# Delta-rule attention followed by a rational feed-forward layer: VectorE's steps of a unit in two fixed blocks of three, and three first halves per chunk made on ScalarE

## The chip, the core and the metric

The kernel runs on one core of a Trainium2 chip. The number that counts is the device time of one execution in microseconds (us). Of the kernel before, three runs are shown: 850.73, 851.33 and 855.22 us, so a median of 851.33 us. The profiled execution took 851.73 us.

The engines are named as in the profile: PE (TensorE, matrix products), DVE (VectorE), ACT (ScalarE), POOL (GpSimd) and SP (SyncE, which issues most DMAs). Each works through its own instructions in the order in which they were put there, and waits at an instruction until what that one needs is there.

## What is computed

Four batches with eight heads of 768 tokens and 48 numbers each go through a delta rule; the result, as 3072 tokens of 384 numbers, goes through a feed-forward layer with a rational function in the middle.

```python
k_n = k / (np.linalg.norm(k, axis=-1, keepdims=True) + 1e-06)
for t in range(S):
    kt, vt, bt = (k_n[:, :, t], v[:, :, t], beta[:, :, t, None])
    y[:, :, t] = np.einsum('bhd,bhde->bhe', q[:, :, t], state)
    v_old = np.einsum('bhde,bhd->bhe', state, kt)
    state = state + bt[:, :, :, None] * np.einsum('bhd,bhe->bhde', kt, vt - v_old)
...
h = x @ w_in
P = a[0] + a[1] * h + a[2] * h2 + a[3] * h3
Q = 1.0 + np.abs(b[0]) * np.abs(h) + np.abs(b[1]) * h2
g = P / (Q + 1e-06)
return (g @ w_out).astype(np.float32)
```

## The kernel before, in words

**Chunks.** The 768 tokens are cut into 12 chunks of 64. Within a chunk the delta rule is solved with matrix products; from chunk to chunk a state is carried. Four functions of a chunk run side by side on different chunks: `ahead` (loads, keys normalized), `front` (products of keys, the inverse of a triangle by small steps on DVE, products of queries), `middle` and `back` (the solution, the next state, the outputs, the tokens for the feed-forward layer). "Attention" below means all of them.

**Two halves.** Numbers that go into a product are kept as two numbers of 16 bits: a first half, which is the number rounded, and a second half, which is the rest. `split16` makes both. In the kernel before, three of its calls in each chunk give the first half to POOL (argument `hi`, L226): for the keys and for the queries (`transposed`, tile `kn`, one buffer that both use in turn) and for the key products (`key_products`, tile `gl`). The second half of these three is a subtraction on POOL (L232). The halves in `kn` go out to DRAM by a DMA (`xdk` for keys, `xdq` for queries), and the next first half may only be written into `kn` when that DMA has read it.

**Units.** The feed-forward layer of a chunk has 8 units of 256 inner columns, so there are 96 units. `hidden(n)` makes a bank of 512 columns in PSUM (tile `ph`, two buffers) with 18 matrix products (L806). `numerator(n)` and `quotient(n)` apply the rational function to it, and `accumulate(n)` multiplies it with `w_out` (L869). Letters for the steps of a unit, used from here on:

- ACT: z (L824, from PSUM), u (L828, from PSUM), |w| (L829), Ln (L842), Exp (L843)
- DVE, each with one input in PSUM and one in SBUF: W (L826, from z and `ph`), U (L830, from u and `ph`), V (L831)
- DVE, each with both inputs in SBUF: G (L848, or L846 where POOL has helped), X (L849), Y (L853)
- POOL: the last product of a unit (L854) in all 96; in 36 units (chunks 2 to 10, units 0, 4, 5 and 6 of each) also L835, just after V, and L851, in place of Y

z(n) comes before W(n), that before u(n) (ACT waits for it in the built program, since both read the same bank), u(n) before U(n), then V(n), G(n) (which also needs Exp(n)), X(n), Y(n) and L854(n).

**Order.** The main loop writes `numerator(n)`, then `quotient(n - 1)`, then a piece of attention, `accumulate(n - 2)` and `hidden(n + 1)`. That order is only a priority: a scheduler that runs when the kernel is built picks for each engine, by its own estimates of durations, the most urgent instruction that would be ready. It may therefore put U(n) behind X(n - 1), or attention between any two steps, and the order that it finds is fixed in the program.

Of the kernel before, what the change touches and what calls it, by code (L numbers as in the profile page):

```python
# [15 lines left out]
ALU = mybir.AluOpType  # L16
# [20 lines left out]
def kernel(  # L37
# [12 lines left out]
    nc = tc.nc  # L50
# [4 lines left out]
    C = 64  # L55
# [120 lines left out]
    def zeroed(n, shape, dtype, nm, part=lambda t: t, eng=nc.gpsimd):  # L176
        made = []
        for i in range(n):
# [14 lines left out]
            eng=nc.vector if nm in "kwe" else nc.gpsimd,  # L193
# [15 lines left out]
    def as_rows(ap, b):  # L209

        return (
            ap[b * C : (b + 1) * C]
            .rearrange("(m j) x -> m (j x)", j=NB)[:, : C * C]
            .rearrange("m (t s) -> t m s", s=C)
        )
# [4 lines left out]

    S16 = cpool.tile([P, HP, D], F32, name="S16")

    def split16(dst, src, scale=None, eng=None, hi=None):

        if hi is not None:
            hi.tensor_scalar(dst[0], src, 1.0 if scale is None else scale, 0.0, op0=ALU.mult, op1=ALU.add)  # L226
        elif scale is None:
            nc.scalar.copy(dst[0], src)  # L228
        else:
            nc.scalar.activation(dst[0], src, AF.Copy, scale=scale)  # L230
        if scale is None:
            (eng or nc.vector).tensor_sub(dst[1], src, dst[0])  # L232
        else:
            nc.vector.scalar_tensor_tensor(  # L234
                out=dst[1], in0=src, scalar=scale, in1=dst[0], op0=ALU.mult, op1=ALU.subtract
            )
# [94 lines left out]
    def load_in(i):  # L331
        w64 = moe_w_in.bitcast(U32)
        t = w_out[:, i].rearrange("p a b e -> p (a b e)").bitcast(U32).rearrange("p (c f) -> p c f", c=NCC)
        for cc in range(NCC):
            to_f32(t[:, cc], w64[cc * P : (cc + 1) * P, i * 4 * P : (i + 1) * 4 * P], f"i{i}_{cc}")
        s2 = w_in[:, i, 0].bitcast(BF16)
        nc.scalar.activation(s2, t.bitcast(F32), AF.Square)
        pf = ps_h.tile([P, 2 * P], F32, tag="h", name=f"pfw{i}")
        for cc in range(NCC):
            nc.tensor.matmul(pf, ones16, s2[:, cc], start=cc == 0, stop=cc == NCC - 1)  # L340
        ss = sb.tile([P, 1], F32, tag="ss", name=f"wss_{i}")
        nc.vector.tensor_reduce(sw[:, 2, i : i + 1], pf, axis=AX.X, op=ALU.max)
# [69 lines left out]
    def bank(pool, nm, w):  # L412

        t = pool.tile([P, NPAIR, 512], F32, tag="a", name=nm)[:, :, : H * w].rearrange("x p (h w) -> x p h w", w=w)
        return t[:, 0], t[:, 1], t

    def by_pair(t):

        return t.rearrange("x (p h) d -> x p h d", p=NPAIR)
# [30 lines left out]
    def transposed(x, src, nm, soon):  # L450


        split16(
            [x[:, i, :, :, :D].rearrange("p h b d -> p b h d") for i in range(2)],
            src.rearrange("p (b h) d -> p b h d", b=2),
            eng=nc.gpsimd,
            hi=nc.gpsimd,
        )
        xd = dpool.tile([NPAIR, 2, NH, C, HG, 2, DP], F16, tag="xd" + nm[0], name=f"xd{nm}", bufs=4 if nm[0] == "k" else 2)
        for p in PAIRS:  # L460
            nc.sync.dma_start(
                out=xd[p].rearrange("i n t a b d -> t (i n) (a b d)"),
                in_=x[p * C : (p + 1) * C].rearrange("t i (n a) b d -> t (i n) (a b d)", n=NH),
            )
        t = sb.tile([P, NPAIR, 2, NH, C, HG], F16, tag="tt", name="t" + nm)
        if soon:
            pts = ps_f.tile([P, 2, H, P], F16, tag="a", name=f"pt{nm}")
            for i in range(2):
                pt = pts[:, i]
                for h in range(H):  # L470
                    nc.tensor.transpose(pt[:, h], x[:, i, h].rearrange("p b d -> p (b d)"), ident16)
                for p in PAIRS:
                    nc.scalar.copy(
                        t[:, p, i].rearrange("x n t a -> x n a t"),
                        pt[:, :, p * C : (p + 1) * C].rearrange("x (n a) t -> x n a t", a=HG),
                    )
            return t, xd
        nc.sync.dma_start(
            out=t.rearrange("x p i n t a -> x (p i n t a)"),
            in_=xd.rearrange("p i n t a b d -> (p i n t a) (b d)"),  # L480
            transpose=True,
        )
        return t, xd
# [29 lines left out]
    def key_products(c):  # L513
        d = info[c]
        gd = d["gd"] = dpool.tile([P, BS], F32, tag="gd", name=f"gd_{c}")
        pg = bank(ps_f, f"pg_{c}", C)
        mm3(pg, d["kbd"], d.pop("tk"))
        g = sb.tile([P, HP, C], F32, tag="g", name=f"g_{c}", bufs=1)
        nc.scalar.mul(by_pair(g), pg[2], -1.0)
        for b in range(2):  # L520
            nc.sync.dma_start(out=as_rows(gd, b), in_=g[b * C : (b + 1) * C])
        gl = sb.tile([P, HP, C - 16, 2], F16, tag="gl", name=f"gl_{c}", bufs=1)
        split16([gl[..., i] for i in range(2)], g[:, :, : C - 16], eng=nc.gpsimd, hi=nc.gpsimd)
        d["gl"] = gl

    def inverse(c):
# [110 lines left out]
    def queries_transposed(c):  # L637
        d = info[c]
        qt = d.pop("qt")
        scaled(qt, d["sq"])  # L640
        d["tq"] = transposed(kn_b, qt, f"q_{c}", c == 0)[0]
# [151 lines left out]

    unit = {}
    acc = {}
    obs = {}

    def hidden(n):
# [17 lines left out]
    def numerator(n):  # L816

        c, f2 = divmod(n, NU)
        d = unit[n]
        A3, B1, A1, B0, A0, Q0 = (toks[c]["m"][:, i, f2 : f2 + 1] for i in range(6))  # L820
        ph = d.pop("ph")

        r = z = sb.tile([P, 2, TG], F32, tag="mr", name=f"mr{n}", bufs=MB)
        nc.scalar.activation(z, ph, AF.Abs, scale=B1)  # L824
        w = sb.tile([P, 2, TG], F32, tag="mw", name=f"mw{n}", bufs=MB)
        nc.vector.scalar_tensor_tensor(out=w, in0=z, scalar=B0, in1=ph, op0=ALU.add, op1=ALU.mult)  # L826
        u = sb.tile([P, 2, TG], F32, tag="mu", name=f"mu{n}", bufs=MB)
        nc.scalar.activation(u, ph, AF.Identity, scale=A3, bias=a2)  # L828
        nc.scalar.activation(w, w, AF.Abs)  # L829
        nc.vector.tensor_mul(u, ph, u)  # L830
        nc.vector.scalar_tensor_tensor(out=u, in0=u, scalar=A1, in1=ph, op0=ALU.add, op1=ALU.mult)  # L831

        by_pool = 2 <= c < NCH - 1 and f2 in (0, 4, 5, 6)
        if by_pool:
            nc.gpsimd.tensor_scalar(u, u, A0, 1.0, op0=ALU.add, op1=ALU.mult)  # L835
        d.update(u=u, w=w, r=r, A0=A0, Q0=Q0, by_pool=by_pool)

    def quotient(n):

        d = unit[n]  # L840
        u, w, r, A0, Q0, by_pool = (d.pop(x) for x in ("u", "w", "r", "A0", "Q0", "by_pool"))
        nc.scalar.activation(r, w, AF.Ln, bias=Q0)  # L842
        nc.scalar.activation(r, r, AF.Exp, scale=-1.0)  # L843
        g = sb.tile([P, 2, 2, TG], F16, tag="mg", name=f"mg{n}", bufs=MB)
        if by_pool:
            nc.vector.tensor_mul(g[:, 0], u, r)  # L846
        else:
            nc.vector.scalar_tensor_tensor(out=g[:, 0], in0=u, scalar=A0, in1=r, op0=ALU.add, op1=ALU.mult)  # L848
        nc.vector.scalar_tensor_tensor(out=w, in0=w, scalar=Q0, in1=g[:, 0], op0=ALU.add, op1=ALU.mult)  # L849
        if by_pool:  # L850
            nc.gpsimd.tensor_sub(u, u, w)  # L851
        else:
            nc.vector.scalar_tensor_tensor(out=u, in0=u, scalar=A0, in1=w, op0=ALU.add, op1=ALU.subtract)  # L853
        nc.gpsimd.tensor_mul(g[:, 1], u, r)  # L854
        d["g"] = g

# [65 lines left out]
    def front(c, j):  # L922

        if j == 0:
            keys_transposed(c)
        elif j == 1:
            key_products(c)
        elif j == 2:
            invs[c] = inverse(c)
            next(invs[c])  # L930
            scales(c)
            queries_transposed(c)
        elif j == 3:
# [113 lines left out]
```

## Time and profile before

| | |
|---|---|
| median of three runs | 851.33 us |
| profiled execution | 851.73 us |
| its span, first to last instruction | 849.4 us |
| first W of unit 0 starts | 150.8 us |
| first W of the last chunk (unit 88) starts | 804.9 us |
| DMA queue of SP, share of 16 engines | 69.7% |
| granted TensorE clock, mean | 0.89 |

In a row of a group of instructions stand the line, the engine, the operation, what it writes and reads, the shape and the count; behind the first bar its busy time in us and the mean duration of one in ns; behind the second bar the idle time of the engine just before these instructions, and what ended most of it. In a row of the timeline stand the start and the duration in us, and in brackets the idle time before it and what ended that. The rows of stretches of time give, for each engine, its busy time and its count of instructions, then the granted clock, the share of the DMA engines that were busy and the GB/s.

### The profile page before, as it was taken

What the parts mean: (1) busy time and instruction counts of PE and PEld (TensorE: products, weight loads), DVE (VectorE), ACT (ScalarE), POOL (GpSimd) and SP (SyncE); (2) the same over time, 40 slices, a digit from 0 to 9 for tenths busy, and PEclk for the clock granted to TensorE, in tenths of its full rate; (3) what the DMA queues carried; (4) which work ended last, traced back from release to release, by engine and by line L of the source; (5) the groups of instructions that cost most, each with busy time, mean ns of one, the idle gap of its engine ahead of it and who ended that gap; (6) DMA issues with size and microseconds to landing.
All of it is one profiled execution on the core that took longest, in us unless ns stands there. A gap on an engine that the chain in (4) does not pass through costs nothing.

```text
span 849.4 us, 23212 instructions
## 1 busy us (share of the span) xinstructions
PE 625.6 (74%) x9264; PEld 491.3 (58%) x9264; DVE 761.0 (90%) x1369; ACT 589.5 (69%) x1242; POOL 466.9 (55%) x430
## 2 busy tenths in 40 slices
PE   0230425777788678888868869879879889999885
PEld 0220425656466467666756747657657767787563
DVE  5999898799799889889978898897999999999886
ACT  3766667748575675886774866767677867887774
POOL 7665665464436556565564655664756546454522
PEclk9855556988999899999999989989989999999999
DMA  8987989959899968959879498379587583300000
GB/s 230 259 198 148 221 157 172 149 117 148 155 172 147 175 123 160 151 102 193 144 140 176 85 183 149 66 158 165 89 159 129 97 139 58 72 2 20 1 20 19
DMA packets 466507, 111.46 MB, mean 131 GB/s; under 512 B 431328, under 2 KB 463072, under 8 KB 466400
## 3 DMA queue, kind: packets, MB, share of 16 engines
q1 hardware_dynamic: 464224, 108.83, 69.7%
q8 instruction: 72, 1.18, 0.6%
q10 hardware_dynamic: 2176, 1.17, 0.5%
q14 instruction: 35, 0.29, 0.1%
HBM read 40.47 MB, written 26.23 MB: 79 GB/s over the span
## 4 chain that ended last, share of the span: by engine, by line
DVE 41%; ACT 14%; DMA 12%; PE 11%; issue 8%; SPq 8%; POOL 3%; POOLq 0%; ACTq 0%; DVEq 0%
DVE mw L849 4%; PE ph L806 4%; PE po L869 4%; DVE w_out L327 3%; DVE mw L826 3%; DVE mg L848 3%; DVE mu L830 3%; DVE mu L831 3%; DVE mu L853 2%; ACT mu L828 2%; DVE mg L846 2%; SPq L609 2%; DVE z L234 2%; ACT mr L824 2%; ACT kp L764 2%
## 5 line engine op out<-in xcount | busy, mean ns | idle before, releaser
L806 PE MATMUL ph<-xT,w_in 128*128 128x256 f16 x1728 | 224.2, 283 | 37.1 <-DVE mu L831 33.8
L869 PE MATMUL po<-w_out,mg 128*128 128x384 f16 x1152 | 223.4, 339 | 33.5 <-POOL mg L854 27.3
L806 PEld LDWEIGHTS <-w_in 128*128 128x128 f16 x1728 | 172.0, 102 | 76.4 <-DVE mu L831 24.9
L854 POOL TENSOR_TENSOR mg<-mu,mr 128x512 f16<-128x512 f32 x96 | 135.3, 1410 | 106.5 <-DVE mu L853 50.9
L869 PEld LDWEIGHTS <-mg 128*128 128x128 f16 x1152 | 110.6, 101 | 105.5 <-POOL mg L854 34.1
L828 ACT ACTIVATE mu<-ph,coef,msc 128x512 f32<-128x512 f32 x96 | 74.7, 778 | 54.4 <-DVE mw L826 54.2
L849 DVE SCALAR_TENSOR_TENSOR mw<-mw,msc,mg 128x512 f32<-128x512 f32 x96 | 92.6, 965 | 0.5
L851 POOL TENSOR_TENSOR mu<-mu,mw 128x512 f32<-128x512 f32 x36 | 51.0, 1418 | 72.5 <-DVE mw L849 38.3
L824 ACT ACTIVATE mr<-ph,msc 128x512 f32<-128x512 f32 x96 | 64.9, 682 | 36.9 <-POOL mg L854 11.5
L403 PEld LDWEIGHTS <-kbd 128*128 128x128 f16 x1680 | 60.8, 104 | 35.2 <-issue 33.4
L826 DVE SCALAR_TENSOR_TENSOR mw<-mr,msc,ph 128x512 f32<-128x512 f32 x96 | 70.4, 737 | 10.7 <-ACT mr L824 10.6
L831 DVE SCALAR_TENSOR_TENSOR mu<-mu,msc,ph 128x512 f32<-128x512 f32 x96 | 70.8, 739 | 1.1
L830 DVE TENSOR_TENSOR mu<-ph,mu 128x512 f32<-128x512 f32 x96 | 65.2, 680 | 5.6 <-ACT mu L828 4.6
L842 ACT ACTIVATE mr<-mw,msc 128x512 f32<-128x512 f32 x96 | 69.4, 724 | 0.9
L403 PE MATMUL pu<-z,ebd 128*128 128x48 f16 x1728 | 52.7, 186 | 19.4 <-DVE z L234 15.4
L848 DVE SCALAR_TENSOR_TENSOR mg<-mu,msc,mr 128x512 f16<-128x512 f32 x60 | 58.9, 982 | 6.2 <-ACT mr L843 5.7
L403 PEld LDWEIGHTS <-ebd 128*128 128x128 f16 x1728 | 51.7, 98 | 22.0 <-issue 20.8
L843 ACT ACTIVATE mr<-mr 128x512 f32<-128x512 f32 x96 | 60.2, 630 | 0.7
L829 ACT ACTIVATE mw<-mw 128x512 f32<-128x512 f32 x96 | 60.0, 625 | 0.0
L853 DVE SCALAR_TENSOR_TENSOR mu<-mu,msc,mw 128x512 f32<-128x512 f32 x60 | 52.1, 869 | 0.2
L835 POOL TENSOR_SCALAR mu<-mu,msc 128x512 f32<-128x512 f32 x36 | 28.1, 782 | 40.5 <-DVE mu L831 28.3
L232 POOL TENSOR_TENSOR mm<-m,mm 128x1024 f16<-128x1024 f32 x12 | 31.1, 2589 | 32.7 <-ACT mm L228 30.5
(198 smaller groups left out, 1306.3 us busy)
## 6 DMA issues: line engine op xcount, KB each, us to landing
wsi<-in_moe_w_in_dram SPq DMA_DIRECT2D x24, 256.0 KB, 5.2
xdk<-kn SPq DMA_DIRECT2D x24, 256.0 KB, 3.7
kbd<-tk SPq DMA_DIRECT2D x24, 256.0 KB, 5.1
gd<-g SPq DMA_DIRECT2D x24, 256.0 KB, 3.5
wso<-in_moe_w_out_dram SPq DMA_DIRECT2D x32, 192.0 KB, 4.0
xdq<-kn SPq DMA_DIRECT2D x24, 256.0 KB, 3.6
mbd<-mm SPq DMA_DIRECT2D x24, 256.0 KB, 5.4
wc<-img SPq DMA_DIRECT2D x24, 256.0 KB, 4.8
```

What stands on the lines that cost most here:

```text
L403: nc.tensor.matmul(dst[p][:, h], head(bd, lp, p * H + h), head(rt, rp, p * H + h), start=start and n == 0 and h == 0, stop=stop and n == l ...
L806: nc.tensor.matmul(ph[:, i], w_in[:, f2, wp, cc, i * P : (i + 1) * P], x[:, xp, cc], start=k == 0, stop=k == 3 * NCC - 1,)
L824: nc.scalar.activation(z, ph, AF.Abs, scale=B1)
L826: nc.vector.scalar_tensor_tensor(out=w, in0=z, scalar=B0, in1=ph, op0=ALU.add, op1=ALU.mult)
L828: nc.scalar.activation(u, ph, AF.Identity, scale=A3, bias=a2)
L830: nc.vector.tensor_mul(u, ph, u)
L831: nc.vector.scalar_tensor_tensor(out=u, in0=u, scalar=A1, in1=ph, op0=ALU.add, op1=ALU.mult)
L842: nc.scalar.activation(r, w, AF.Ln, bias=Q0)
L848: nc.vector.scalar_tensor_tensor(out=g[:, 0], in0=u, scalar=A0, in1=r, op0=ALU.add, op1=ALU.mult)
L849: nc.vector.scalar_tensor_tensor(out=w, in0=w, scalar=Q0, in1=g[:, 0], op0=ALU.add, op1=ALU.mult)
L854: nc.gpsimd.tensor_mul(g[:, 1], u, r)
L869: nc.tensor.matmul(po[p], g[:, gp, i, p * P : (p + 1) * P], w_out[:, f2, wp, i], start=f2 == lo and i == 0 and k == 0, stop=f2 == hi - 1 a ...
```

## The change

The change does two things. The six DVE steps of a unit get a mark, by which the scheduler has to leave them in the order in which the program writes them: W, U, V of unit n, then G, X, Y of unit n - 1 (where POOL helps, there is no Y). Anything else may still be put between them. And the argument `hi` is gone, so that the three first halves per chunk are made by ACT; POOL keeps the second halves.

```diff
-    def split16(dst, src, scale=None, eng=None, hi=None):
-
-        if hi is not None:
-            hi.tensor_scalar(dst[0], src, 1.0 if scale is None else scale, 0.0, op0=ALU.mult, op1=ALU.add)
-        elif scale is None:
+    def split16(dst, src, scale=None, eng=None):
+
+        if scale is None:
             nc.scalar.copy(dst[0], src)
...
             src.rearrange("p (b h) d -> p b h d", b=2),
             eng=nc.gpsimd,
-            hi=nc.gpsimd,
         )
...
-        split16([gl[..., i] for i in range(2)], g[:, :, : C - 16], eng=nc.gpsimd, hi=nc.gpsimd)
+        split16([gl[..., i] for i in range(2)], g[:, :, : C - 16], eng=nc.gpsimd)
...
+    def in_order(bi):
+
+        tc.stamp_issue_order_token(bi.ins, "unit")
+
...
-        nc.vector.scalar_tensor_tensor(out=w, in0=z, scalar=B0, in1=ph, op0=ALU.add, op1=ALU.mult)
+        in_order(nc.vector.scalar_tensor_tensor(out=w, in0=z, scalar=B0, in1=ph, op0=ALU.add, op1=ALU.mult))
...
-        nc.vector.tensor_mul(u, ph, u)
-        nc.vector.scalar_tensor_tensor(out=u, in0=u, scalar=A1, in1=ph, op0=ALU.add, op1=ALU.mult)
+        in_order(nc.vector.tensor_mul(u, ph, u))
+        in_order(nc.vector.scalar_tensor_tensor(out=u, in0=u, scalar=A1, in1=ph, op0=ALU.add, op1=ALU.mult))
...
         if by_pool:
-            nc.vector.tensor_mul(g[:, 0], u, r)
+            in_order(nc.vector.tensor_mul(g[:, 0], u, r))
         else:
-            nc.vector.scalar_tensor_tensor(out=g[:, 0], in0=u, scalar=A0, in1=r, op0=ALU.add, op1=ALU.mult)
-        nc.vector.scalar_tensor_tensor(out=w, in0=w, scalar=Q0, in1=g[:, 0], op0=ALU.add, op1=ALU.mult)
+            in_order(nc.vector.scalar_tensor_tensor(out=g[:, 0], in0=u, scalar=A0, in1=r, op0=ALU.add, op1=ALU.mult))
+        in_order(nc.vector.scalar_tensor_tensor(out=w, in0=w, scalar=Q0, in1=g[:, 0], op0=ALU.add, op1=ALU.mult))
...
-            nc.vector.scalar_tensor_tensor(out=u, in0=u, scalar=A0, in1=w, op0=ALU.add, op1=ALU.subtract)
+            in_order(nc.vector.scalar_tensor_tensor(out=u, in0=u, scalar=A0, in1=w, op0=ALU.add, op1=ALU.subtract))
```

Two places show what the scheduler made of it. The first is DVE's order near the end, in the last chunk, where no attention is left; the digits behind `mw`, `mu` and `mg` are the unit's number. Before, it stood so:

```order
L826 SCALAR_TENSOR_TENSOR mw91_13902<-mr91_13900,msc_11_13624,ph_91_13881 128x512
L849 SCALAR_TENSOR_TENSOR mw90_13853<-mw90_13853,msc_11_13624,mg90_13911 128x512
L853 SCALAR_TENSOR_TENSOR mu90_13855<-mu90_13855,msc_11_13624,mw90_13853 128x512
L830 TENSOR_TENSOR mu91_13904<-ph_91_13881,mu91_13904 128x512
L831 SCALAR_TENSOR_TENSOR mu91_13904<-mu91_13904,msc_11_13624,ph_91_13881 128x512
L826 SCALAR_TENSOR_TENSOR mw92_13949<-mr92_13947,msc_11_13624,ph_92_13928 128x512
L848 SCALAR_TENSOR_TENSOR mg91_13958<-mu91_13904,msc_11_13624,mr91_13900 128x512
L849 SCALAR_TENSOR_TENSOR mw91_13902<-mw91_13902,msc_11_13624,mg91_13958 128x512
L830 TENSOR_TENSOR mu92_13951<-ph_92_13928,mu92_13951 128x512
```

With the change (whose lines have moved down by two: L828, L832, L833, L850, L851 and L855 are W, U, V, G, X and Y) the same place reads:

```order
L828 SCALAR_TENSOR_TENSOR mw91_13902<-mr91_13900,msc_11_13624,ph_91_13881 128x512
L832 TENSOR_TENSOR mu91_13904<-ph_91_13881,mu91_13904 128x512
L833 SCALAR_TENSOR_TENSOR mu91_13904<-mu91_13904,msc_11_13624,ph_91_13881 128x512
L850 SCALAR_TENSOR_TENSOR mg90_13911<-mu90_13855,msc_11_13624,mr90_13851 128x512
L851 SCALAR_TENSOR_TENSOR mw90_13853<-mw90_13853,msc_11_13624,mg90_13911 128x512
L855 SCALAR_TENSOR_TENSOR mu90_13855<-mu90_13855,msc_11_13624,mw90_13853 128x512
L828 SCALAR_TENSOR_TENSOR mw92_13949<-mr92_13947,msc_11_13624,ph_92_13928 128x512
L832 TENSOR_TENSOR mu92_13951<-ph_92_13928,mu92_13951 128x512
```

Between W and U of one unit there stood two steps of the unit before; now U is right behind W, and G has moved behind the V of the next unit. Over the whole program W and U have nothing between them in 22 of 96 units (before in 1) and a single instruction in 23 (before in 5). Pairs in which a step directly follows the one whose result it reads (U and V, G and X, X and Y) were 49 and are 115.

The second place is the first halves in `kn` for the queries of chunk 6 and the keys of chunk 7. Before, both stood in POOL's order, between the units' steps:

```order
L226 TENSOR_SCALAR kn0_109<-q_6_5318 128x2x8x48
L851 TENSOR_TENSOR mu24_5619<-mu24_5619,mw24_5617 128x512
L232 TENSOR_TENSOR kn0_109<-q_6_5318,kn0_109 128x2x8x48
L854 TENSOR_TENSOR mg24_5754<-mu24_5619,mr24_5615 128x512
L854 TENSOR_TENSOR mg25_6007<-mu25_5747,mr25_5743 128x512
L232 TENSOR_TENSOR rr_5_6277<-v_5_4061,rr_5_6277 128x768
L226 TENSOR_SCALAR kn0_109<-k_7_5424 128x2x8x48
```

With the change they stand in ACT's order (L826, L830, L831, L844 and L845 are now z, u, |w|, Ln and Exp):

```order
L226 CAST kn0_109<-q_6_5318 128x2x8x48
L826 ACTIVATE mr24_5615<-ph_24_5596,msc_3_5316 128x512
L826 ACTIVATE mr25_5743<-ph_25_5724,msc_3_5316 128x512
L830 ACTIVATE mu24_5619<-ph_24_5596,coef_99,msc_3_5316 128x512
L831 ACTIVATE mw24_5617<-mw24_5617 128x512
L844 ACTIVATE mr24_5615<-mw24_5617,msc_3_5316 128x512
L845 ACTIVATE mr24_5615<-mr24_5615 128x512
L226 CAST kn0_109<-k_7_5424 128x2x8x48
L830 ACTIVATE mu25_5747<-ph_25_5724,coef_99,msc_3_5316 128x512
```

The first half of the keys, which has to wait until the queries' DMA has left `kn`, is now in front of u of unit 25 on ACT.

## The prediction, made before the changed kernel ran

> **What bounds the kernel now.** I read the page's busy times first, then the chain that ended last, and then the stretches of time.
>
> ```profile
> span 849.4 us, 23212 instructions
> PE 625.6 (74%) x9264; PEld 491.3 (58%) x9264; DVE 761.0 (90%) x1369; ACT 589.5 (69%) x1242; POOL 466.9 (55%) x430
> DVE 41%; ACT 14%; DMA 12%; PE 11%; issue 8%; SPq 8%; POOL 3%; POOLq 0%; ACTq 0%; DVEq 0%
> ```
>
> DVE is busy for 90% of the span and has the largest share of the chain; ACT has 260 us of idle time, POOL 383. The stretches below are the chunks 0 to 8, the chunks 9 and 10, and the last chunk with the end.
>
> ```profile
> 150.80:721.30 570.50, 469.20 (x7366) 369.81 (x7365) 518.81 (x857) 398.30 (x810) 322.56 (x261) 0.93 0.79 138
> 721.30:804.90 83.60, 78.94 (x972) 61.00 (x969) 76.12 (x118) 67.98 (x135) 40.76 (x34) 1.00 0.11 25
> 804.90:849.40 44.50, 31.27 (x212) 20.61 (x210) 34.15 (x48) 26.59 (x43) 10.96 (x9) 0.93 0.07 18
> ```
>
> In the first of them DVE (third pair) works 91% of the time; in the second PE (94%) and DVE (91%) are both nearly full. So a microsecond more or less in DVE's queue is mostly one in the span. How much of DVE's time is work? The groups of the unit's steps answer that.
>
> ```profile
> L849 DVE SCALAR_TENSOR_TENSOR mw<-mw,msc,mg 128x512 f32<-128x512 f32 x96 | 92.6, 965 | 0.5
> L831 DVE SCALAR_TENSOR_TENSOR mu<-mu,msc,ph 128x512 f32<-128x512 f32 x96 | 70.8, 739 | 1.1
> L826 DVE SCALAR_TENSOR_TENSOR mw<-mr,msc,ph 128x512 f32<-128x512 f32 x96 | 70.4, 737 | 10.7 <-ACT mr L824 10.6
> L830 DVE TENSOR_TENSOR mu<-ph,mu 128x512 f32<-128x512 f32 x96 | 65.2, 680 | 5.6 <-ACT mu L828 4.6 <-POOL mm L232 0.7
> L848 DVE SCALAR_TENSOR_TENSOR mg<-mu,msc,mr 128x512 f16<-128x512 f32 x60 | 58.9, 982 | 6.2 <-ACT mr L843 5.7
> L853 DVE SCALAR_TENSOR_TENSOR mu<-mu,msc,mw 128x512 f32<-128x512 f32 x60 | 52.1, 869 | 0.2
> L846 DVE TENSOR_TENSOR mg<-mu,mr 128x512 f16<-128x512 f32 x36 | 32.7, 908 | 5.1 <-ACT mr L843 4.3 <-POOL mu L835 0.7
> L854 POOL TENSOR_TENSOR mg<-mu,mr 128x512 f16<-128x512 f32 x96 | 135.3, 1410 | 106.5 <-DVE mu L853 50.9
> L851 POOL TENSOR_TENSOR mu<-mu,mw 128x512 f32<-128x512 f32 x36 | 51.0, 1418 | 72.5 <-DVE mw L849 38.3
> ```
>
> W, U and V read `ph` in PSUM and take 737, 680 and 739 ns. G, X and Y, of the same size, read two tiles in SBUF and take 0.87 to 0.98 us. The timeline shows why.
>
> ```profile
> 641.95 2.37 POOL L232 TENSOR_TENSOR mm<-m,mm 128x1024 f16<-128x1024 f32 x1 [1.01 <-ACT mm L228]
> 642.02 2.85 DVE L849 SCALAR_TENSOR_TENSOR mw<-mw,msc,mg 128x512 f32<-128x512 f32 x1
> 649.10 0.73 DVE L849 SCALAR_TENSOR_TENSOR mw<-mw,msc,mg 128x512 f32<-128x512 f32 x1
> ```
>
> The same X takes 0.73 us, or 2.85 us when POOL began a subtraction 0.07 us earlier; then it ends 0.55 us after POOL does. So a DVE step with two SBUF inputs stands still while POOL runs, and one that reads PSUM doesn't. What this costs: X 96 x (0.965 - 0.74) = 21.6 us, L848 60 x (0.982 - 0.74) = 14.5, L853 60 x (0.869 - 0.74) = 7.7, L846 36 x (0.908 - 0.68) = 8.2; together **52 us**, the most that an order of the unit's steps can win there.
>
> A rule of the Trainium skill bears on this ("SBUF — State Buffer", section "SBUF: two separate sides"): VectorE and GpSimd share one pair of ports as an exclusive lock, and the loser is blocked for the other's whole instruction; on VectorE's side two SBUF inputs are enough to need it. The rows above agree (2.85 against 0.73 us). The rule speaks for blocks, since in a PSUM block POOL is free, and against them as well, since in a block of G, X, Y any POOL step that arrives gets in at a boundary and stops the next. With no collision left the sum below would be 32 us lower, which is the first rival's way.
>
> **The change part by part.** (a) *The unit's own POOL steps.* L854 follows Y, so after the change it runs beside W, U, V of the next unit, and L851 likewise. They are 135.3 + 51.0 = 186.3 us of the 374.3 us that POOL is busy in the three stretches, so by share 26 of the 52 us. I take **-20**, as the steps of attention are longer (2.37 us above) and stop DVE longer. Bounds 0 and -52.
>
> (b) *36 first halves leave POOL.*
>
> ```profile
> L226 POOL TENSOR_SCALAR gl<-g 128x768 f16<-128x768 f32 x12 | 13.4, 1119 | 8.4 <-ACT g L519 8.0
> L226 POOL TENSOR_SCALAR kn<-k 128x768 f16<-128x768 f32 x12 | 11.3, 944 | 21.1 <-DMA xdq<-kn 21.0
> L226 POOL TENSOR_SCALAR kn<-q 128x768 f16<-128x768 f32 x12 | 10.9, 912 | 0.7
> L228 ACT CAST rr<-v 128x768 f16<-128x768 f32 x12 | 9.9, 828 | 10.0 <-DVE v L679 10.0
> ```
>
> At the rate of (a), 26 us for 132 steps or 0.2 us each, that is **-7** (bounds 0 and -15).
>
> (c) *G no longer waits for Exp.* It now stands a unit later. Its 5.7 + 4.3 us of waits go: **-10** (bounds -5 and -10). Late next is z, for which W already waits 10.6 us.
>
> (d) *L835 gets between G and X.* It is released by V, and G(n - 1) is now the step behind V.
>
> ```profile
> 645.45 0.74 DVE L853 SCALAR_TENSOR_TENSOR mu<-mu,msc,mw 128x512 f32<-128x512 f32 x1
> 645.70 1.05 POOL L835 TENSOR_SCALAR mu<-mu,msc 128x512 f32<-128x512 f32 x1 [1.38 <-DVE mu L831]
> L835 POOL TENSOR_SCALAR mu<-mu,msc x36: 691/696/1408, 302.2 to 796.7; 128x512 f32<-128x512 f32 x36
> ```
>
> It came 0.25 us into a Y, waited for that (1.05 instead of 0.70 us) and ended 0.56 us behind it. X, which follows its G at once, would be held for about 0.33 us net, in 36 units: **+12** (bounds 0 and 36 x 0.70 = 25).
>
> (e) *DVE has nothing between W and U.* The timeline near the end shows the loop.
>
> ```profile
> 826.89 0.75 DVE L826 SCALAR_TENSOR_TENSOR mw<-mr,msc,ph 128x512 f32<-128x512 f32 x1 [0.45 <-ACT mr L824]
> 827.56 0.74 DVE L848 SCALAR_TENSOR_TENSOR mg<-mu,msc,mr 128x512 f16<-128x512 f32 x1
> 827.67 0.78 ACT L828 ACTIVATE mu<-ph,coef,msc 128x512 f32<-128x512 f32 x1 [0.81 <-DVE mw L826]
> 828.34 0.75 DVE L849 SCALAR_TENSOR_TENSOR mw<-mw,msc,mg 128x512 f32<-128x512 f32 x1
> 829.00 0.68 DVE L830 TENSOR_TENSOR mu<-ph,mu 128x512 f32<-128x512 f32 x1
> 829.60 0.74 DVE L853 SCALAR_TENSOR_TENSOR mu<-mu,msc,mw 128x512 f32<-128x512 f32 x1
> 830.92 0.74 DVE L826 SCALAR_TENSOR_TENSOR mw<-mr,msc,ph 128x512 f32<-128x512 f32 x1
> ```
>
> W ends at 827.64, u runs on ACT from 827.67 to 828.45, and G and X fill that time, so that a unit takes 830.92 - 826.89 = 4.03 us. In the new order U is next behind W: it can start at 828.49 at the earliest, 1.60 us after W, where the next step otherwise starts 0.66 us after the one before. That is 0.94 us lost, and all that stands behind U waits with it. In the built order 22 units have nothing in between (21 us) and 36 more have steps that by the trace's durations are shorter than 0.94 us, and lose 17 us; before, the same count gives 6 us. So **+31** (bounds +15, the empty ones less 6, and +45, where ACT is not free when W ends). 7.5 us of it lie in the last chunk, where nothing else is left to fill.
>
> (f) *Neighbours that depend on each other.* G at 827.56 ends at 828.30 and X, which reads it, starts 0.04 us later; X ends at 829.09, but U, which doesn't read it, starts 0.09 us before that. The difference is 0.12 us, and 66 such pairs are added: **+8** (bounds 0 and +8). The Trainium skill ("VectorE: DVE Perf Modes", section "The DRAIN you can't avoid") reports eight copies that took the same with a semaphore after each as with one at the end; by that (f) would be 0 and the sum 8 us lower. The trace has this difference, so I keep it.
>
> (g) *ACT's 36 first halves.* At 828 ns, the row for `rr`, they are 30 us, beside 260 us of idle time. But the 21.0 us that POOL waited for `xdq` to leave `kn` move to ACT with them, and behind the keys' half stands the u that DVE needs.
>
> ```profile
> 429.97 0.83 POOL L226 TENSOR_SCALAR kn<-q 128x768 f16<-128x768 f32 x1
> 442.45 0.83 POOL L226 TENSOR_SCALAR kn<-k 128x768 f16<-128x768 f32 x1 [3.35 <-DMA xdq<-kn]
> 491.93 0.82 POOL L226 TENSOR_SCALAR kn<-q 128x768 f16<-128x768 f32 x1
> 500.82 0.83 POOL L226 TENSOR_SCALAR kn<-k 128x768 f16<-128x768 f32 x1 [3.92 <-DMA xdq<-kn]
> ```
>
> From the queries' half to the free buffer it took 12.5 and 8.9 us. In the built order 4.5 to 6.9 us of ACT work lie between the two in seven chunks. DVE can go on for some 3 us with the steps of the unit before, so I take 2 us in each of seven: **+14** (bounds 0 and 11 x 3.6 = 40, the waits above in all eleven).
>
> (h) *Absorbed.* DVE idles 698.6 - 629.1 = 69.5 us in the three stretches, waiting for attention that doesn't run faster when DVE is late; a tenth of that swallows delay: **-7** (bounds 0 and -15). The first 150.8 us hold no unit; I count nothing for them.
>
> The sum: -20 - 7 - 10 + 12 + 31 + 8 + 14 - 7 = +21 us. The span becomes 849.4 + 21 = 870.4, and with the 2.3 us around it (851.73 - 849.4) **872.7 us**. The profiled execution is 0.4 us above the median of 851.33, so nothing has to be shifted.
>
> **The rivals.**
>
> *POOL's collisions vanish (faster).* If POOL's steps of attention also fall into the PSUM blocks, which (e) makes longer, (a) becomes three quarters of the 52 us, -39; a gap in which POOL works off its queue also spares collisions, so (d) is 0, (e) is 20 and (g) 8. The sum is -39 - 7 - 10 + 20 + 8 + 8 = -20: 832 us. For it speaks the size of the 52 us; against it, that releases of POOL's attention steps have no tie to the blocks. With the other terms as I took them, the sign turns where (a) passes 41 us.
>
> *They cancel (no change).* (a) -30 and (g) +6 with the rest as above give +3: 855 us.
>
> *ACT holds everything up.* (g) at its bound of 40 gives +47: 899 us. In order, ACT would stop u, z and Exp for each late DMA. DVE's slack of 3 us speaks against it.
>
> *The blocks don't do what they say.* POOL's steps run late and land in G, X, Y as often as before; (a) is 0: +41, 893 us.
>
> **How the numbers follow.** My forecast, 860 to 886 us, has a chance of 0.45; the faster rival 0.25; the cancelling one 0.13; ACT 0.10; the blocks without effect 0.07. The predicted time is 873 us. A measurement of this kernel can tell a change from none at about 0.5%, 4 us. Faster has 0.25, the same 0.13, slower 0.45 + 0.10 + 0.07 = 0.62. The range reaches from 832, the faster rival's time, to 897, short of the worst of ACT: about 0.12 and 0.07 are left out.
>
> **What would show it.** Right, if X's mean falls from 965 ns towards 800 and L854's idle time before it stays; if U's idle time, ended by u (L828), grows from 4.6 us to 30 or more; if a unit in the last chunk takes 5.2 us (1.60 + 0.72 + 0.66 + 0.78 + 0.78 + 0.66) instead of 4.03; if ACT's halves in `kn` show a wait for `xdq` of 14 us or more. Wrong, if U doesn't wait (ACT's u came without W, or the gaps were filled), if G, X and Y fall to 0.75 us all over, or if the chain turns to PE.

## The result, and the profile after

The changed kernel takes **878.42 us** (median of 4 runs, 876.82 to 880.06), beside 853.28 us for the kernel before (4 runs, the three shown above and one of 855.31 us): a ratio of 1.0321, 95% interval 1.0288 to 1.0353. It is slower, by 25 us. The forecast was 873.0 us, with 832 to 897 as its range. The traces are of single executions: 879.89 us for the changed kernel and 851.73 us for the kernel before, so their difference is about 3 us larger than that of the medians.

The page of the changed kernel, its span, its busy times and its chain:

```profile
span 878.2 us, 23202 instructions
PE 640.3 (73%) x9264; PEld 500.0 (57%) x9264; DVE 743.7 (85%) x1369; ACT 615.6 (70%) x1278; POOL 428.0 (49%) x394
DVE 40%; DMA 18%; PE 14%; SPq 10%; ACT 8%; issue 6%; POOL 2%; POOLq 0%; DVEq 0%; ACTq 0%
```

DVE works *less* than before (743.7 us, before 761.0) and still the span is 28.8 us longer: DVE's idle time went from 849.4 - 761.0 = 88.4 to 878.2 - 743.7 = 134.5 us, by 46.1. The groups of instructions say where; W, U, V, G, X, Y are now L828, L832, L833, L850 (with POOL's help L848), L851 and L855, and POOL's steps L837, L853 and L856.

```profile
L851 DVE SCALAR_TENSOR_TENSOR mw<-mw,msc,mg 128x512 f32<-128x512 f32 x96 | 88.3, 920 | 1.0
L828 DVE SCALAR_TENSOR_TENSOR mw<-mr,msc,ph 128x512 f32<-128x512 f32 x96 | 70.9, 739 | 1.7 <-ACT mr L826 1.6
L832 DVE TENSOR_TENSOR mu<-ph,mu 128x512 f32<-128x512 f32 x96 | 65.9, 686 | 47.1 <-ACT mu L830 43.0 <-POOL mg L856 2.3 <-POOL rr L230 1.6
L850 DVE SCALAR_TENSOR_TENSOR mg<-mu,msc,mr 128x512 f16<-128x512 f32 x60 | 48.2, 803 | 0.0
L855 DVE SCALAR_TENSOR_TENSOR mu<-mu,msc,mw 128x512 f32<-128x512 f32 x60 | 47.8, 797 | 1.1
L848 DVE TENSOR_TENSOR mg<-mu,mr 128x512 f16<-128x512 f32 x36 | 25.6, 711 | 0.0
L837 POOL TENSOR_SCALAR mu<-mu,msc 128x512 f32<-128x512 f32 x36 | 37.4, 1039 | 53.3 <-DVE mu L833 53.1
```

G, X and Y together took 92.6 + 58.9 + 52.1 + 32.7 = 236.3 us before and take 88.3 + 48.2 + 47.8 + 25.6 = 209.9 now: the collisions with POOL did fall, by 26.4 us. The idle time before U went from 5.6 to 47.1 us, that before W from 10.7 to 1.7, and that before G from 6.2 + 5.1 to nothing. That is +41.5 - 9.0 - 11.3 = +21.2 of the 46.1 us; the other 24.9 stand nearly all before steps of attention. Some of the waits (what waits, for what, us in total, times, longest) name them:

```profile
DVE mu L832 <- ACT mu L830: 43.0, 45, 2.9
...
ACT kn L226 <- DMA xdq<-kn: 25.7, 7, 7.8
...
DVE sc L617 <- PE pfq L247: 7.0, 5, 2.3
DVE nrm L492 <- ACT sq L491: 7.0, 4, 2.7
DVE xs L737 <- PE px L736: 6.0, 4, 2.0
...
DVE m L655 <- PE pm L401: 4.6, 5, 1.3
```

DVE waits for u in 45 units, about 0.96 us each. ACT's wait for the queries' DMA is the second row; what it costs DVE is a question for the runs. The last chunk's timeline shows the new loop:

```profile
856.91 0.74 DVE L828 SCALAR_TENSOR_TENSOR mw<-mr,msc,ph 128x512 f32<-128x512 f32 x1
857.68 0.78 ACT L830 ACTIVATE mu<-ph,coef,msc 128x512 f32<-128x512 f32 x1 [2.14 <-DVE mw L828]
858.57 0.69 DVE L832 TENSOR_TENSOR mu<-ph,mu 128x512 f32<-128x512 f32 x1 [0.92 <-ACT mu L830]
859.29 0.75 DVE L833 SCALAR_TENSOR_TENSOR mu<-mu,msc,ph 128x512 f32<-128x512 f32 x1
859.96 0.75 DVE L850 SCALAR_TENSOR_TENSOR mg<-mu,msc,mr 128x512 f16<-128x512 f32 x1
860.74 0.75 DVE L851 SCALAR_TENSOR_TENSOR mw<-mw,msc,mg 128x512 f32<-128x512 f32 x1
861.53 0.75 DVE L855 SCALAR_TENSOR_TENSOR mu<-mu,msc,mw 128x512 f32<-128x512 f32 x1
862.20 0.74 DVE L828 SCALAR_TENSOR_TENSOR mw<-mr,msc,ph 128x512 f32<-128x512 f32 x1
```

W, then u on ACT, then U, each after the other: 862.20 - 856.91 = 5.29 us a unit, where the kernel before took 4.03.

### The profile page after: what moved, and what is told of

The parts are those of the page before. It is cut to its first block, busy times and chain, and to the rows that moved or that the text cites. A ratio compares the mean times of both kernels' runs of the same rounds, so it can differ in the third digit from the quotient of the medians.

```text
span 878.2 us, 23202 instructions
## 1 busy us (share of the span) xinstructions
PE 640.3 (73%) x9264; PEld 500.0 (57%) x9264; DVE 743.7 (85%) x1369; ACT 615.6 (70%) x1278; POOL 428.0 (49%) x394
## 4 chain that ended last, share of the span: by engine, by line
DVE 40%; DMA 18%; PE 14%; SPq 10%; ACT 8%; issue 6%; POOL 2%; POOLq 0%; DVEq 0%; ACTq 0%
DVE mw L851 5%; PE ph L808 4%; DVE mu L833 4%; DVE mu L832 4%; PE po L871 4%; DMA k<-in_k_dram 3%; DVE mw L828 3%; DVE w_out L325 3%; ACT mu L830 3%; DVE mg L850 3%; DMA gb<-gd 3%; DVE mu L855 2%; SPq L119 2%; SPq L606 2%; DMA tk<-xdk 2%
## 5 line engine op out<-in xcount | busy, mean ns | idle before, releaser
L808 PE MATMUL ph<-xT,w_in 128*128 128x256 f16 x1728 | 228.7, 289 | 54.3 <-DVE mu L833 52.4
L808 PEld LDWEIGHTS <-w_in 128*128 128x128 f16 x1728 | 175.0, 104 | 98.9 <-DVE mu L833 37.5
L856 POOL TENSOR_TENSOR mg<-mu,mr 128x512 f16<-128x512 f32 x96 | 126.5, 1318 | 132.6 <-DVE mu L855 112.3
L871 PEld LDWEIGHTS <-mg 128*128 128x128 f16 x1152 | 107.2, 100 | 96.5 <-POOL mg L856 33.8
L830 ACT ACTIVATE mu<-ph,coef,msc 128x512 f32<-128x512 f32 x96 | 74.3, 774 | 83.7 <-DVE mw L828 83.5
L832 DVE TENSOR_TENSOR mu<-ph,mu 128x512 f32<-128x512 f32 x96 | 65.9, 686 | 47.1 <-ACT mu L830 43.0
L851 DVE SCALAR_TENSOR_TENSOR mw<-mw,msc,mg 128x512 f32<-128x512 f32 x96 | 88.3, 920 | 1.0
L401 PEld LDWEIGHTS <-kbd 128*128 128x128 f16 x1680 | 64.3, 107 | 34.9 <-issue 32.5
L853 POOL TENSOR_TENSOR mu<-mu,mw 128x512 f32<-128x512 f32 x36 | 45.9, 1275 | 67.5 <-DVE mw L851 46.1
L833 DVE SCALAR_TENSOR_TENSOR mu<-mu,msc,ph 128x512 f32<-128x512 f32 x96 | 71.4, 744 | 1.9
L828 DVE SCALAR_TENSOR_TENSOR mw<-mr,msc,ph 128x512 f32<-128x512 f32 x96 | 70.9, 739 | 1.7 <-ACT mr L826 1.6
L844 ACT ACTIVATE mr<-mw,msc 128x512 f32<-128x512 f32 x96 | 68.9, 718 | 0.7
L826 ACT ACTIVATE mr<-ph,msc 128x512 f32<-128x512 f32 x96 | 64.9, 679 | 5.7 <-PE ph L808 2.4
L837 POOL TENSOR_SCALAR mu<-mu,msc 128x512 f32<-128x512 f32 x36 | 37.4, 1039 | 53.3 <-DVE mu L833 53.1
L845 ACT ACTIVATE mr<-mr 128x512 f32<-128x512 f32 x96 | 60.2, 627 | 0.8
L401 PEld LDWEIGHTS <-ebd 128*128 128x128 f16 x1728 | 51.2, 98 | 16.6 <-issue 13.3
L831 ACT ACTIVATE mw<-mw 128x512 f32<-128x512 f32 x96 | 59.6, 621 | 0.0
L401 PEld LDWEIGHTS <-wbd 128*128 128x128 f16 x1152 | 35.6, 100 | 29.7 <-issue 25.8
L855 DVE SCALAR_TENSOR_TENSOR mu<-mu,msc,mw 128x512 f32<-128x512 f32 x60 | 47.8, 797 | 1.1
```

Of the source, the lines that this page charges most:

```text
L401: nc.tensor.matmul(dst[p][:, h], head(bd, lp, p * H + h), head(rt, rp, p * H + h), start=start and n == 0 and h == 0, stop=stop and n == l ...
L808: nc.tensor.matmul(ph[:, i], w_in[:, f2, wp, cc, i * P : (i + 1) * P], x[:, xp, cc], start=k == 0, stop=k == 3 * NCC - 1,)
L828: in_order(nc.vector.scalar_tensor_tensor(out=w, in0=z, scalar=B0, in1=ph, op0=ALU.add, op1=ALU.mult))
L832: in_order(nc.vector.tensor_mul(u, ph, u))
L833: in_order(nc.vector.scalar_tensor_tensor(out=u, in0=u, scalar=A1, in1=ph, op0=ALU.add, op1=ALU.mult))
L851: in_order(nc.vector.scalar_tensor_tensor(out=w, in0=w, scalar=Q0, in1=g[:, 0], op0=ALU.add, op1=ALU.mult))
```

## The experiments

Twelve kernels ran. "U" and "W" are DVE's idle time just before these steps, "G, X, Y" the busy time of the four groups of rows (184.3 us if nothing disturbed them, by the prediction's 236.3 less 52), all from the one profiled execution of each (its steps' records added up), which need not be a typical one (that of e3 took 844.72 us, that of e6 870.33, the shortest of their runs); "unit" is the time of one in the last chunk. Each ratio is to runs of the kernel before on the same chip. A "free" order is one without the marks; "halves" says which engine makes the three first halves.

| kernel | order | halves | us | ratio to before, 95% interval | U | W | G, X, Y | unit |
|---|---|---|---|---|---|---|---|---|
| before | free | POOL | 853.28 | | 5.6 | 10.7 | 236.3 | 4.03 |
| after | W U V, G X Y | ACT | 878.42 | 1.0321 [1.0288, 1.0353] | 47.1 | 1.7 | 209.9 | 5.29 |
| e1 | W U V, G X Y | POOL | 884.47 | 1.0388 [1.0346, 1.0430] | 55.8 | 0.6 | 226.1 | 5.29 |
| e2 | free | ACT | 852.34 | 1.0010 [0.9986, 1.0033] | 11.0 | 11.4 | 230.9 | 4.03 |
| e3 | as after, u ahead of W | ACT | 850.46 | 1.0003 [0.9975, 1.0032] | 0.0 | 18.4 | 231.3 | 4.28 |
| e4 | as after, u ahead of W | POOL | 854.50 | 1.0036 [1.0013, 1.0059] | 0.0 | 23.0 | 229.6 | 4.28 |
| e5 | W, G X, U V, Y | ACT | 847.62 | 0.9955 [0.9927, 0.9983] | 1.0 | 8.0 | 229.8 | 4.82 |
| e6 | as after | ACT, keys POOL | 873.56 | 1.0279 [1.0209, 1.0349] | 52.3 | 1.4 | 221.2 | 5.29 |
| e7 | as e3 | ACT, keys POOL | 850.21 | 0.9984 [0.9952, 1.0016] | 0.0 | 25.0 | 231.8 | 4.28 |
| e8 | free, u ahead of W | ACT | 859.64 | 1.0076 [1.0030, 1.0122] | 0.0 | 22.0 | 235.7 | uneven |
| e9 | U V W(n+1), G X Y(n-1) | ACT | 902.35 | 1.0594 [1.0569, 1.0619] | 1.4 | 83.8 | 210.6 | 5.18 |
| e10 | as e5 | POOL | 855.21 | 1.0063 [1.0037, 1.0089] | 1.6 | 7.8 | 244.5 | 4.82 |
| e11 | U V W(n+1), G X Y(n) | ACT | **831.09** | 0.9755 [0.9723, 0.9786] | 2.5 | 13.3 | 208.5 | 4.28 |
| e12 | free, written as e11 | ACT | 872.37 | 1.0231 [1.0191, 1.0272] | 10.4 | 11.4 | 245.0 | 4.03 |

### Each half of the change alone

e1 keeps the marks and gives the halves back to POOL; e2 takes the marks away.

```diff
e1:
             eng=nc.gpsimd,
+            hi=nc.gpsimd,
...
e2:
-        tc.stamp_issue_order_token(bi.ins, "unit")
+        return bi
```

> The blocks alone: W, U, V and G, X, Y keep their fixed order, and POOL makes the three first halves per chunk again, as before. If the order is what costs (the empty time between W and U, terms (e) and (f), less the collisions and Exp waits that it saves), the time lies 12 to 22 us above before, U's idle time stays at 40 us or more, and a unit of the last chunk stays at 5.3 us. If the halves on ACT are what costs (ACT held up by the queries' DMA, 25.7 us of waits in the changed kernel), the time is within 5 us of before.

> The halves alone: ACT makes the three first halves, and the unit's steps are free to be ordered as before. If the order is what costs, the time lies 3 to 10 us above before (ACT's waits for the queries' DMA, less POOL's collisions), a unit of the last chunk takes 4.0 us. If the halves are what costs, it lies 20 us or more above before. If the two parts add up, the differences of this run and of the order alone make up the 25 us of both.

The order alone costs 3.9%, the halves alone nothing that can be told from zero. So the loss belongs to the order. Both runs missed what was expected of them: e1 is 34 us above before, not 12 to 22, and e2 lies at most 3 us above, not 3 to 10. The two parts don't add up either, since 3.9% and 0.1% stand beside 3.2% for both together. Within the fixed order, ACT's halves are a gain, 884.47 to 878.42 us, though the intervals of the two ratios just overlap.

### The empty time between W and U taken away

e3 writes u ahead of W. Neither reads what the other makes, so u needn't wait for W; ACT now makes it first, and the blocks, the marks and ACT's halves stay. e4 is the same with the halves on POOL.

```diff
-        w = sb.tile([P, 2, TG], F32, tag="mw", name=f"mw{n}", bufs=MB)
-        in_order(nc.vector.scalar_tensor_tensor(out=w, in0=z, scalar=B0, in1=ph, op0=ALU.add, op1=ALU.mult))
         u = sb.tile([P, 2, TG], F32, tag="mu", name=f"mu{n}", bufs=MB)
         nc.scalar.activation(u, ph, AF.Identity, scale=A3, bias=a2)
+        w = sb.tile([P, 2, TG], F32, tag="mw", name=f"mw{n}", bufs=MB)
+        in_order(nc.vector.scalar_tensor_tensor(out=w, in0=z, scalar=B0, in1=ph, op0=ALU.add, op1=ALU.mult))
```

> The changed kernel with u written ahead of W, so that ACT makes z and u one after the other, W waits for u, and U can follow W at once. The arithmetic is the same. If the empty time between W and U is the loss, U's idle time falls from 47 us to under 10, a unit of the last chunk takes 4.3 us (0.66 + 0.66 + 0.72 + 0.66 + 0.78 + 0.78) instead of 5.3, and the kernel falls to 835 to 850 us. If the wait only moves in front of W (z and u together late) the time stays above 865 us.

> Blocks, u ahead of W, and the three first halves on POOL as before. Against the run with u ahead of W and the halves on ACT it tells what the halves do when the empty time is gone: if ACT held up by the queries' DMA is a loss, this one is 3 to 15 us faster; if POOL's collisions are worth more, it is slower by up to 7 us.

The groups of e3 (W is L830 there), and its timeline in the last chunk:

```profile
L851 DVE SCALAR_TENSOR_TENSOR mw<-mw,msc,mg 128x512 f32<-128x512 f32 x96 | 88.6, 923 | 1.0
L830 DVE SCALAR_TENSOR_TENSOR mw<-mr,msc,ph 128x512 f32<-128x512 f32 x96 | 71.1, 741 | 18.4 <-ACT mu L828 16.4 <-POOL kn L230 1.5 <-issue 0.4
L832 DVE TENSOR_TENSOR mu<-ph,mu 128x512 f32<-128x512 f32 x96 | 65.5, 682 | 0.0
```

```profile
805.68 0.74 DVE L830 SCALAR_TENSOR_TENSOR mw<-mr,msc,ph 128x512 f32<-128x512 f32 x1
806.34 0.69 DVE L832 TENSOR_TENSOR mu<-ph,mu 128x512 f32<-128x512 f32 x1
807.07 0.75 DVE L833 SCALAR_TENSOR_TENSOR mu<-mu,msc,ph 128x512 f32<-128x512 f32 x1
...
809.96 0.74 DVE L830 SCALAR_TENSOR_TENSOR mw<-mr,msc,ph 128x512 f32<-128x512 f32 x1
```

U starts 0.66 us after W, and W now waits for u: 47.1 + 1.7 us of idle time at the two steps became 18.4. The time falls from 878.42 to 850.46 us, by 28.0 (by the ratios, which allow for the runs of before beside each, by 3.2%, or 27 us); 835 to 850 was expected. A unit takes 809.96 - 805.68 = 4.28 us, 0.25 more than before. G, X and Y, however, are back at 231.3 us. DVE's busy time as a whole isn't: it is 742.3 us, beside 743.7 in the changed kernel, since DVE's steps of attention took about 14 us less in e3.

### ACT's wait for the queries' DMA

e6 and e7 are the changed kernel and e3, with the keys' first half alone on POOL, so that ACT no longer waits for `kn` to be read.

```diff
...
+            hi=nc.gpsimd if nm[0] == "k" else None,
```

> The changed kernel with the first half of the keys back on POOL; ACT keeps those of the queries and of the key products. So ACT no longer waits for the queries' DMA (25.7 us of waits in the changed kernel). If those waits delay u and so DVE, as term (g) had it at 14 us, the time falls to 860 to 870 us. If DVE has work of its own in them (it was idle for 3.3 us in them by the trace), the time stays within 4 us of the changed kernel, 874 to 883 us.

> Blocks, u ahead of W, ACT makes the halves of queries and key products, POOL those of the keys. Lies between the two runs with u ahead of W (850.5 with all halves on ACT, 854.5 with all on POOL): 846 to 856 us. Under 846 would say that ACT's wait for the queries' DMA does cost once DVE has no empty time.

ACT's wait is gone (POOL has it now, 23.8 us in both runs). The time falls by 4.9 us in e6 (873.56, between the two ranges that were expected), with intervals that overlap, and by 0.2 in e7. In the trace of the changed kernel DVE is idle for 3.3 us within the 25.7 us of ACT's wait, so nearly all of that wait is covered while it lasts. What the wait costs in all the two runs don't say: e6 takes it away, but with POOL's 12 steps back, G, X and Y rise from 209.9 to 221.2 us, and its 4.9 us are what is left of both; in e7 they don't rise (231.3 and 231.8), but there the wait that was taken away was only 10.9 us long in e3.

### Other fixed orders, and a free one with u ahead

e5 fixes the order W(n), G, X(n - 1), U, V(n), Y(n - 1), near to what the scheduler had chosen before; e10 is that with the halves on POOL. e8 is e3 without the marks. The changes are `yield` statements between the steps, and in the main loop:

```diff
-            numerator(n)
...
-            quotient(n - 1)
+        next(num, None)
+        next(quo, None)
+        next(num, None)
+        next(quo, None)
+        next(num, None)
```

> The changed kernel with another fixed order, written out step by step: W(n), G(n-1), X(n-1), U(n), V(n), Y(n-1). Two steps of the unit before stand between W and U, as the free order had them near the end, and there are no blocks. If the empty time between W and U is the loss, and not that the order is fixed, U's idle time is under 10 us, G, X and Y collide with POOL again (45 us or more above their undisturbed time, against 24 in the changed kernel), and the time is 846 to 860 us. If a fixed order costs by itself, because the scheduler can't move a late step, it stays above 866 us.

> The fixed order W, G, X, U, V, Y with the three first halves back on POOL. Against the same order with the halves on ACT (847.6 us) it shows what the halves are worth in an order without the gap: 2 to 8 us slower if POOL's 36 steps collide as before; within 2 us if ACT's load takes back what POOL's collisions cost; faster if ACT's waits for the queries' DMA hold u up.

> u ahead of W and the halves on ACT, but the order of the unit's steps free. Beside the run with blocks and u ahead of W (850.5) it tells what the blocks themselves are worth once W and U need no gap. If blocks spare collisions, this one is 3 to 10 us slower than that; if the free order is as good, it is within 3 us (847 to 854); if u ahead of W helps the free order by itself, it falls under 845.

A fixed order isn't a loss as such: e5 is 0.5% faster than the kernel before. ACT's halves are worth 7.6 us in it (855.21 against 847.62; by the ratios 9). And with u ahead, the marks are worth 9 us (e8 859.64, e3 850.46; by the ratios 6).

### W a unit ahead

e9 puts W of the next unit in U's block, so that z, W and u have a whole block's time between them.

```diff
         in_order(nc.vector.scalar_tensor_tensor(out=w, in0=z, scalar=B0, in1=ph, op0=ALU.add, op1=ALU.mult))
+        yield
...
-            numerator(n)
+            next(num, None)
+        if n + 1 < N:
+            num = numerator(n + 1)
+            next(num)
...
-            hidden(n + 1)
+            hidden(n + 2)
```

> Blocks of three again, halves on ACT, but each block on PSUM is U(n), V(n), W(n+1): W stands one unit ahead, so that G, X, Y stand between W and its U, and u stays behind W as in the kernel before. Tables of scalars for units 4 to 7 are made one unit earlier for it. If the empty time between W and U is the loss and blocks as such are not, U's idle time is under 5 us, a unit of the last chunk takes 4.3 us, and the time is 835 to 852 us. If blocks lose in another way (more neighbours that depend on each other, POOL held off), it stays above 858 us.

It was the slowest of all. U's idle time went as the expectation had it for a loss by the empty time, to 1.4 us, and the loss came by a way that neither of its branches had named. The waits tell which:

```profile
DVE mw L828 <- ACT mr L826: 83.6, 55, 7.2
ACT mr L826 <- POOL mg L857: 58.9, 42, 3.2
```

z (L826) of the unit ahead writes into `mr`, which has three buffers, and the one that it needs is still read by POOL's last product (L857) of an earlier unit. The empty time moved from U to W and grew from 47.1 to 83.8 us.

### W a unit ahead, with G, X, Y of the unit itself

e11 keeps that order of U, V, W and takes G, X, Y of unit n instead of n - 1, so that `mr` comes free a unit earlier. e12 is the same text without the marks.

```diff
-        if 0 <= n - 1 < N:
-            quotient(n - 1)
+        if n < N:
+            quotient(n)
...
-        if 0 <= n - 2 < N:
-            accumulate(n - 2)
+        if 0 <= n - 1 < N:
+            accumulate(n - 1)
```

> The changed kernel with other blocks: U, V of unit n, then W of unit n + 1, then G, X, Y of unit n itself (not of the unit before), all marked. So between W and U of one unit stand G, X, Y (2.2 us), z of the next unit only needs a free buffer that the last product on POOL of two units earlier has read, and the last product of a unit runs beside U, V, W. accumulate and the attention tables come a unit earlier. The two dependent neighbours of a block stay. Theory 1 (the loss of the change is the empty time between W and U, the blocks are no loss): idle time before U under 8 us, before W under 15 us, before G up to 15 us (G now needs its own Exp, with one W of 0.7 us in between instead of a unit), a unit in the last chunk of 4.2 to 4.6 us, and 838 to 856 us. Theory 2 (blocks of three lose, wherever ACT's step stands, as 902 us with W one unit ahead suggested): above 870 us, with the wait now at G (Ln and Exp of the same unit) or at z (POOL's last product). The rule that empty time on VectorE keeps POOL off G, X, Y expects their excess at 45 us or more, as with the other orders without a gap.

> The kernel of the run before (U, V of unit n, W of unit n + 1, then G, X, Y of unit n, everything a unit earlier) without the marks: the same text, but the scheduler chooses the order. It tells whether the 831 us came from the fixed blocks or from writing G, X, Y for their own unit. Theory 1 (the blocks: no step waits for another engine's step of the same block, and few POOL steps fall into G, X, Y): 842 to 856 us, like the other free orders (851 before, 852 with the halves on ACT), with the excess of G, X and Y back at 40 to 50 us. Theory 2 (what is written, not the marks): 828 to 838 us, with an excess of G, X and Y under 30 us.

The page of e11, and then its groups (U, V, W, G, X, Y are L833, L834, L828, L851 or L849, L852, L856):

```profile
span 829.5 us, 23205 instructions
PE 621.0 (75%) x9264; PEld 489.1 (59%) x9264; DVE 729.3 (88%) x1369; ACT 615.4 (74%) x1278; POOL 412.6 (50%) x394
```

```profile
L852 DVE SCALAR_TENSOR_TENSOR mw<-mw,msc,mg 128x512 f32<-128x512 f32 x96 | 74.9, 780 | 1.2
L828 DVE SCALAR_TENSOR_TENSOR mw<-mr,msc,ph 128x512 f32<-128x512 f32 x96 | 70.9, 739 | 13.3 <-ACT mr L826 12.9
L833 DVE TENSOR_TENSOR mu<-ph,mu 128x512 f32<-128x512 f32 x96 | 65.4, 682 | 2.5 <-ACT mu L831 2.5
L851 DVE SCALAR_TENSOR_TENSOR mg<-mu,msc,mr 128x512 f16<-128x512 f32 x60 | 54.2, 903 | 1.4 <-ACT mr L846 1.2
L849 DVE TENSOR_TENSOR mg<-mu,mr 128x512 f16<-128x512 f32 x36 | 27.4, 761 | 7.8 <-POOL mu L838 7.1 <-ACT mr L846 0.7
L838 POOL TENSOR_SCALAR mu<-mu,msc 128x512 f32<-128x512 f32 x36 | 25.0, 695 | 8.3 <-DVE mu L834 7.1 <-DVE sf L741 0.2
```

This one beats both kernels: 831.09 us, 2.4% below the kernel before, and below the 838 us that the better of its two theories had allowed. Without the marks the same text takes 872.37 us, more than either theory had said: the scheduler's own orders alone lie between 851 (before) and 872 us. The groups of e12:

```profile
L852 DVE SCALAR_TENSOR_TENSOR mw<-mw,msc,mg 128x512 f32<-128x512 f32 x96 | 92.3, 964 | 0.4
L833 DVE TENSOR_TENSOR mu<-ph,mu 128x512 f32<-128x512 f32 x96 | 65.3, 682 | 10.4 <-ACT mu L831 10.1
L856 DVE SCALAR_TENSOR_TENSOR mu<-mu,msc,mw 128x512 f32<-128x512 f32 x60 | 60.1, 1003 | 0.2
L851 DVE SCALAR_TENSOR_TENSOR mg<-mu,msc,mr 128x512 f16<-128x512 f32 x60 | 58.1, 970 | 4.3 <-ACT mr L846 3.6
```

Between the two profiled executions lie 870.6 - 829.5 = 41.1 us; DVE's busy time is 768.0 - 729.3 = 38.7 us of that, and G, X, Y are 36 of it. In this order blocks of three do what they were meant to do: POOL falls into G, X and Y far less. X needs 780 ns here, 964 there. It isn't so in every order: with u ahead, the blocks of e3 have 231.3 us beside 235.7 in the free order of e8.

This also ends a theory of mine. After e3 and e5, in which G, X and Y grew back to 230 us once the gap was gone, I took the empty time itself for what had kept POOL away. e11 has no such gap (DVE idles 100.2 us, as in e3 with 100.7) and G, X, Y at 208.5. What sets e3 apart from e11 isn't settled. One part is seen: L837 (L838 in e11) starts beside G in 31 of its 36 times in e3, and never beside G, X or Y in e11, where 20 times it starts beside W, which reads PSUM. By the trace it costs G and X 5.6 us there and no collision here; but here L849, which reads what it makes, waits 7.1 us for it (the row above). The rest of the 23 us lies with steps of attention (`mm`, `kn`, `rr`) and the last product.

## Why the prediction was right where it was, and where not

The sign and its cause were right, the size 5 us low. By groups of terms, for the profiled executions (28.8 us of span; the last row but one is what the others leave over):

| terms | forecast | measured |
|---|---|---|
| (a), (b), (d): G, X, Y and POOL | -15 | -26.4 |
| (c): G and Exp | -10 | -11.3 |
| (e): empty time, U with W | +31 | +32.5 |
| (f): dependent neighbours | +8 | about +8 |
| (g), (h): ACT's wait, absorbed | +7 | the rest, +26 |
| sum | +21 | +28.8 |

**(e) was right, and is shown.** The wait is the one forecast (u, 45 units), the last chunk has 5.29 us a unit where 5.2 was said, and e3, whose edit only turns u and W round, gives 28.0 us back. Two other fixed orders without this wait, e5 and e11, lose nothing either. (The parts of (e), 21 and 17 less 6, add up to 32, not 31.)

**(f) was right.** In e3 and e11 a unit without a wait has three dependent neighbours (U to V, G to X, X to Y) where the loop before had one; it takes 4.28 instead of 4.03 us, or 0.125 for each of the two, against 0.12 in the forecast. It also explains 5 of the 9.1 us by which DVE's busy time fell less (17.3 us) than G, X and Y did (26.4): independent neighbours overlap in the records by about 0.08 us (862.20 lies before 861.53 + 0.75), and 66 such overlaps were lost. If the eight copies of the Trainium skill ("VectorE: DVE Perf Modes", section "The DRAIN you can't avoid"), which took as long with a semaphore after each as with one at the end, held for these steps, the unit would have stayed at 4.03; it didn't.

**(c) was right**: the wait before G went to zero.

**(a) was over-sized, (b) under-sized, (d) over-sized.** The order alone (e1) took G, X, Y from 236.3 to 226.1, so (a) with (d) was -10, near the forecast of -8. But L835 cost 4.5 us in the trace after and about 6 in that of e1, not 12, so (a) itself was about -15 or -16, not -20. X's mean, which was to fall from 965 ns towards 800, stopped at 920. ACT's halves took another 16 us off G, X, Y (226.1 to 209.9) where I had -7; in the time 6 of them were left (e1 to after), and nothing in a free order (e2).

**(g) is not borne out, and its size stays open.** The wait went to ACT as said (25.7 us, forecast 14 or more), but while it lasted DVE had other work: 3.3 us of idle time lie in it, so that "2 us in each of seven", taken as time in which DVE stands empty during the wait, was too much; the steps of the unit before, which I counted as cover, covered nearly all of it. A cost that comes later isn't excluded, since e6 mixes it with 11.3 us of collisions. What can be told is the sum of (b) and (g): +7 in the forecast, and 6 us of gain from e1 to the changed kernel.

**(h) had the wrong sign.** I let attention's idle time swallow 7 us of delay. Instead DVE's idle time before other steps than W, U and G grew by 24.9 us. Before attention's steps it is the waits for PE that grew, from 3.6 to 24.2 us (`sc`, `xs` and `m` above are among them), while those for ACT stayed at 29. PE for its part waited 52.4 us for V to leave `ph`, before 33.8. Whether the one makes the other isn't shown, and why the waits grew is open. It isn't the empty time alone, since in e1, with more of it, these gaps are where they were before (51.2 us before attention's steps, before 51.6, after 74.2). With the keys' half on POOL they fall to 49.8 in e6 but not in e7 (75.0; e3 68.8). So neither the empty time nor ACT's wait accounts for them by itself; that they come of both together, in this order, would fit e1 and e6, and no run tests it further.

**The rivals.** The collisions were to vanish: half of the 52 us did, and that wasn't enough against (e). That e11, with collisions like those of the changed kernel and no gap, lies at 831 us, beside this rival's 832, is partly chance, since the rival had nearly all of the 52 us gone. (With no collision left, (d) would be nothing too, and the sum 37 us lower, not the 32 of the prediction.) "Blocks without effect" had G, X and Y at their old time; the order alone (e1) took 10 us off them, so it is wrong for this kernel, but in e3 and e4, the same blocks without the gap, only 5 to 7 us are left of that. "ACT holds everything up" was to cost 40 us by ACT's wait; e6, without that wait, gains 4.9, and 16 even if all that its G, X and Y lost is added.

## What to carry to other kernels

Before an order is fixed, ask of each pair of neighbours whether another engine has a step between them, and how long that takes: here 0.96 us in 45 of 96 units took more than the blocks won, and blocks of the same kind with W a unit earlier and G, X, Y of their own unit gained 2.4% where these lost 3.2%. Then ask the same of buffers, since an order that works further ahead needs its buffers back earlier (e9). And look at busy and idle time apart: the changed kernel had less of the one, and the gain was real, but hidden behind more of the other.

## What the runs showed of the hardware

POOL pays for a collision as well, and the size shows which DVE step stands beside it. The same L835 takes 1039 ns on average in the changed kernel, where G follows V and 32 of the 36 start while G runs, and 695 ns in e11, where W, with an input in PSUM, stands there and none starts beside G, X or Y. The lock that the Trainium skill describes ("SBUF — State Buffer", section "SBUF: two separate sides") agrees with this. That L835 comes between G and X was foreseen; that one PSUM step in that place takes the collision away was not. It doesn't take the whole cost away: G of the same unit is then so near that it waits for L835's result, 7.1 us in e11.
